# The second MoE's output products, pairs 2 and 3: from direct accumulation in PSUM to Strassen products of two quads, summed in SBUF

## The chip, the cores and the metric

One Trainium2 chip, one of its cores. The metric is the device time of one execution, in microseconds. Three timed runs of the kernel before took 842.42, 842.51 and 843.38 us; the profiled execution took 843.36 us. The engines named below: PE multiplies matrices and writes PSUM; DVE (vector), ACT (scalar) and POOL (GpSimd) work on elements; SP issues the DMAs.

## The reference

An attention with softmaxes over q and k and no score matrix, then two feed-forward layers, each 512 to 2048 to 512 over 2304 tokens:

```
q_s = softmax(q, axis=-1);  k_s = softmax(k, axis=seq)
x = q_s @ (k_s.T @ v)                              # 4 x 8 heads, 576 x 64 -> 2304 x 512
x = softplus(x @ moe_w_in) @ moe_w_out             # "first MoE"
out = elu(x @ moe2_w_in) @ moe2_w_out              # "second MoE"
```

All is float32.

## The kernel before

**Tiles.** Tokens go in six blocks of 384 (3 x 128), two blocks to a *pair* (p = 0, 1, 2 in the code, pairs 1 to 3 in the text). The 2048 inner columns go in eight *quads* of 256 (f = 0 to 7). The program is `for m in MoEs: for p in pairs: for f in quads`, 48 quads. Accuracy comes from splitting each float32 operand x into a high part (a cast to fp32r, by ACT) and a low part (x minus the high part, by DVE), and from three matmuls per product: high x high, high x low, low x high.

**Input products** (`add_up`, L791): for one quad and one pair, a Strassen scheme (Winograd's form) of seven products instead of eight, numbered 1, 2, 6, 5, 3, 7, 4 in PE's order. Each is six matmuls of 384 columns (L811) into the banks `ub`, `ua` or `uc`. ACT copies intermediate states of `ub` into `s` tiles (L824), DVE adds them to `ua` and `uc` for h (L845). The seven sums of x ("forms", `add_forms`) are made once per pair, in `xf`; those of w_in once, and for the second MoE they lie in DRAM (`wfd`) and are loaded per quad in pairs 2 and 3.

**Activation** (`add_elu`, L914): ACT computes relu(-h) and exp (L921, L925), DVE subtracts 1 (L929) and takes max(h, 0) + u for g (L933). `add_g` splits g, 768 columns for each of two row groups j, into `gh` (ACT, L940) and `gl` (DVE, L944).

**Output products** (`add_down`, L984): per quad, 2 x 2 x 3 groups of three matmuls of 512 columns (L1016) add to six PSUM banks `acc`, one per 128 tokens, which stay open over all eight quads of a pair. `add_store` then copies the banks out and stores them. A quad's output products are put between the next quad's input products. w_out's high and low parts (`wo`, 1 MB) lie in DRAM (`wod`) and are loaded per quad.

**Order.** Every operation is a *step* with an engine, an assumed duration, its operands and a ring of buffers (`rings`, L207). `Plan.order` plays all steps through once when the program is built and always takes, per engine, the step that can start soonest, ties by how late it may start; a step's lateness comes from due times given to PE's products and from a table of priorities (`PRI`, L1080). The result is one fixed order per engine, and each engine then runs its own instructions strictly in turn.

Of the kernel before, what the change touches and what calls it, by code (L numbers as in the profile page):

```python
# [147 lines left out]
def t_pool(n):  # L148
    return 0.15 + n / 476
# [7 lines left out]
def attention_moe_moe_kernel(  # L157
# [257 lines left out]
    def add_q(t, hps, behind=()):  # L415
# [26 lines left out]
        eng = POOL if early else DVE  # L442

        @step(eng, 1.1 if early else t_dve(n), r=[qm], w=[qk])
        def _(eng=eng):
            (nc.gpsimd if eng == POOL else nc.vector).tensor_tensor(
                flat(), flat(), T[qm][:, :N].to_broadcast([P, N, D]), op=ALU.subtract
            )
# [535 lines left out]
    def add_down(m, p, f):  # L984

        wk = ("wo", m, "o", f) if p == direct(m, 0, f) else ("wo", m, "o", f, p)
        t0 = after_quad(m, p, f)
# [6 lines left out]
        for (i, j, r), at in zip(order, fill):  # L994
# [11 lines left out]
                make=[(ak, f"acc{half}")] if first else [], due=t0 + at + 0.01, line=("acc", half, r),  # L1006
            )
            def _(col=col, j=j, hk=hk, lk=lk, ak=ak, first=first, whole=whole, gk=gk, w32=w32):
# [6 lines left out]
                for n, (g, a) in enumerate(((hk, 0), (hk, 1), (lk, 0))):  # L1015
# [4 lines left out]
                    )  # L1020

    def add_store(m, p):
# [22 lines left out]
        for half in range(2):  # L1045
            for r in range(R):
# [21 lines left out]

                @step(DMA, t_dma(P * DM * 4), r=[sk, ("y2", m)] if both else [sk], w=[] if m else [yk], after=LAT)
# [82 lines left out]

# [37 lines left out]
```

## Time and profile before

| what | value |
|---|---|
| median of three timed runs | 842.51 us |
| profiled execution, its time | 843.36 us |
| its span, first to last instruction | 841.3 us |
| PE busy, share of the span | 821.2 us, 98% |
| weight loads (beside PE) | 721.3 us |
| DVE busy | 590.1 us, 70% |
| ACT busy | 534.2 us, 63% |
| POOL busy | 6.1 us, 1% |
| TensorE clock granted | 0.999 of 2.4 GHz |
| DMA | 186.37 MB, 222 GB/s over the span |

How to read it: a row's duration is how long one instruction was under way. Instructions of one engine overlap, matmuls above all, so what one costs is the distance between starts. Times in windows and timelines count from the span's start. "xN" is a number of instructions.

### The profile page before, as it was taken

How to read it: one execution, taken by the hardware profiler on the slowest of the kernel's cores; microseconds unless marked ns; L12 is line 12 of the kernel's file. 1: busy time of each engine (PE TensorE's matmuls, PEld its weight loads, DVE VectorE, ACT ScalarE, POOL GpSimd, SP SyncE). 2: the span in 40 equal slices, each digit the busy share in tenths (PEclk: the TensorE clock that was granted, in tenths of full speed). 3: DMA queues.
4: the chain of work that ended last, by engine and by line, in shares of the span. 5: the costliest groups of instructions: out<-in, count | busy, mean ns of one | idle time of the engine just before them, and what ended most of it. 6: DMA issues, size and time to landing. Idle time of an engine off the chain costs nothing.

```text
span 841.3 us, 11929 instructions
## 1 busy us (share of the span) xinstructions
PE 821.2 (98%) x4678; PEld 721.3 (86%) x4678; DVE 590.1 (70%) x910; ACT 534.2 (63%) x786; POOL 6.1 (1%) x28
## 2 busy tenths in 40 slices
PE   5799999999999999999999999999999999999998
PEld 4466788889989999999999999899888899888896
DVE  7889999988888768776776786776544556533433
ACT  3877988886887757656655665665534456534443
POOL 2000000000000000000000000000000000000000
PEclk9999999999999999999999999999999999999999
DMA  9687775537885654687756689673765453763532
GB/s 283 165 280 248 216 261 194 199 100 238 263 310 181 236 205 161 221 303 267 250 178 230 261 300 338 257 295 143 250 234 216 179 232 139 255 232 138 187 139 76
DMA packets 63575, 186.37 MB, mean 222 GB/s; under 512 B 17952, under 2 KB 27168, under 8 KB 54560
## 3 DMA queue, kind: packets, MB, share of 16 engines
q1 hardware_dynamic: 63520, 185.61, 63.2%
q8 instruction: 37, 0.61, 0.3%
q14 instruction: 18, 0.15, 0.1%
HBM read 131.07 MB, written 54.53 MB: 221 GB/s over the span
## 4 chain that ended last, share of the span: by engine, by line
PE 83%; DVE 9%; ACT 5%; DMA 2%; issue 2%; ACTq 0%; DVEq 0%; SPq 0%
PE acc L1016 27%; PE ub L811 21%; PE acc L978 15%; PE uc L811 11%; PE ua L811 5%; PE px L507 1%; DMA raw_i<-in_moe_w_in_dram 1%; DMA raw_o<-in_moe_w_out_dram 1%; DVE mt L331 1%; PE pk L375 1%; DVE wf_i L731 1%; PE up L872 1%; ACT kvbd L401 1%; DVE ti_o L655 1%; PE pq L491 1%
## 5 line engine op out<-in xcount | busy, mean ns | idle before, releaser
L811 PE MATMUL ub<-xf,wf_i 128*128 128x384 f32 x1104 | 226.7, 340 | 0.4 <-ACT s L824 0.3
L1016 PE MATMUL acc<-wo_o,gh 128*128 128x512 f32 x720 | 226.0, 395 | 0.0
L811 PEld LDWEIGHTS ub<-xf,wf_i 128*128 128x128 f32 x1104 | 193.4, 188 | 16.5 <-ACT s L824 2.8
L845 DVE TENSOR_TENSOR h<-uc,s 128x384 f32<-128x384 f32 x92 | 51.1, 555 | 143.4 <-PE uc L811 135.0
L1016 PEld LDWEIGHTS acc<-wo_o,gh 128*128 128x128 f32 x720 | 132.5, 188 | 18.8
L1016 PE MATMUL acc<-wo_o,gl 128*128 128x512 f32 x360 | 142.5, 396 | 0.0
L824 ACT COPY s<-ub 128x384 f32<-128x384 f32 x138 | 65.9, 478 | 106.8 <-PE ub L811 106.5
L811 PE MATMUL uc<-xf,wf_i 128*128 128x384 f32 x552 | 112.2, 338 | 0.6 <-ACT g L893 0.6
L978 PE MATMUL acc<-gh,wo_o 128*128 128x512 f32 (+1 forms) x512 | 111.4, 339 | 0.0
L811 PEld LDWEIGHTS uc<-xf,wf_i 128*128 128x128 f32 x552 | 96.6, 188 | 8.2 <-ACT g L893 1.4
L940 ACT CAST gh<-g 128x768 fp32r<-128x768 f32 x92 | 77.1, 839 | 37.8 <-DVE g L933 37.1
L944 DVE TENSOR_TENSOR gl<-g,gh 128x768 fp32r<-128x768 f32 x92 | 87.8, 954 | 18.2 <-ACT gh L940 17.8
L978 PEld LDWEIGHTS acc<-gh,wo_o 128*128 128x128 f32 x512 | 83.2, 188 | 7.1
L1016 PEld LDWEIGHTS acc<-wo_o,gl 128*128 128x128 f32 x360 | 67.5, 187 | 14.4
L978 PE MATMUL acc<-gl,wo_o 128*128 128x512 f32 (+1 forms) x256 | 65.4, 336 | 0.0
L811 PE MATMUL ua<-xf,wf_i 128*128 128x384 f32 x276 | 55.8, 336 | 0.0
L811 PEld LDWEIGHTS ua<-xf,wf_i 128*128 128x128 f32 x276 | 48.0, 188 | 1.4 <-ACT xq L497 0.3
L933 DVE SCALAR_TENSOR_TENSOR g<-h,u 128x768 f32<-128x768 f32 x48 | 45.9, 957 | 1.4
L978 PEld LDWEIGHTS acc<-gl,wo_o 128*128 128x128 f32 x256 | 39.1, 188 | 5.3
L921 ACT ACTIVATE u<-h 128x768 f32<-128x768 f32 x48 | 40.7, 848 | 4.5 <-DVE h L845 2.7
L731 DVE TENSOR_TENSOR wf_i<-st_i,wf_i 128x1024 fp32r<-128x1024 f32 x30 | 36.6, 1221 | 8.1 <-ACT wf_i L727 7.9
L925 ACT ACTIVATE u<-u 128x768 f32<-128x768 f32 x48 | 40.7, 847 | 1.1
(98 smaller groups left out, 937.1 us busy)
## 6 DMA issues: line engine op xcount, KB each, us to landing
wo_o<-wod SPq DMA_DIRECT2D x30, 1024.0 KB, 6.8
wf_i<-wfd SPq DMA_DIRECT2D x16, 1792.0 KB, 7.3
raw_i<-in_moe_w_in_dram SPq DMA_DIRECT2D x16, 1024.0 KB, 6.5
raw_o<-in_moe_w_out_dram SPq DMA_DIRECT2D x16, 1024.0 KB, 7.4
wod<-wo_o SPq DMA_DIRECT2D x16, 1024.0 KB, 6.2
wfd<-wf_i SPq DMA_DIRECT2D x8, 1792.0 KB, 9.0
r_i<-w32i SPq DMA_DIRECT2D x24, 512.0 KB, 5.5
w32i<-ti_i SPq DMA_DIRECT2D x14, 512.0 KB, 5.5
```

What stands on the lines that cost most here:

```text
L331: top = lambda o, x, y: nc.vector.tensor_tensor(o, x, y, op=ALU.max)
L731: nc.vector.tensor_tensor(view(1, lo, n, c), get(), view(0, lo, n, c).bitcast(F32), op=ALU.subtract)
L811: nc.tensor.matmul(ps[:, :BLK], T[wk][:, lo : lo + P], T[xk][:, (2 * c + kc) * BLK : (2 * c + kc + 1) * BLK], start=(i in first and kc == ...
L824: nc.scalar.copy(new(sk), T[key][:, :BLK])
L845: nc.vector.tensor_tensor(T[hk][:, half * BLK : (half + 1) * BLK], T[key][:, :BLK], T[sk], op=ALU.add)
L921: nc.scalar.activation(new(uk), T[hk], AF.Relu, scale=-1.0)
L925: nc.scalar.activation(T[uk], T[uk], AF.Exp, scale=-1.0)
L933: nc.vector.scalar_tensor_tensor(new(gk), T[hk], 0.0, T[uk], op0=ALU.max, op1=ALU.add)
L940: nc.scalar.copy(new(hk), T[gk])
L944: nc.vector.tensor_tensor(new(lk), T[gk], T[hk].bitcast(F32), op=ALU.subtract)
L978: nc.tensor.matmul(ps, T[wk][:, lo : lo + P], T[g][:, cols], start=(first and n == 0 and starts), stop=(f == NQ - 1 and j == 1 and n == 2) ...
L1016: nc.tensor.matmul(ps, T[g][:, col : col + P], T[wk][:, (2 * a + j) * DM : (2 * a + j + 1) * DM], start=(first and n == 0), stop=(f == NQ ...
```

## The change

For pairs 2 and 3 of the second MoE (`fast(m, p)`: m = 1 and p > 0) the output products too become Strassen products, over two quads at a time (step c = 0 to 3, quads 2c and 2c+1):

- `add_g_fast` replaces `add_g`: g stays float32 in its buffer. Per quad POOL makes the sums of its four blocks (four subtractions of 384 columns), ACT and DVE split each of seven forms into a tile `dx`, which takes both quads' parts.
- `add_down_fast` replaces `add_down`: for each form, in the order 1, 2, 6, 5, 3, 7, 4, three groups (one per 128 tokens) of six matmuls of 256 columns into a bank `db`, `da` or `dc`. After each group the bank's present sum is added to half a row of the output in SBUF (`Y`), by DVE, or copied there by ACT where it is the first. Banks `db` and `dc` are written on after that. Rows go to DRAM at the last step; there is no `add_store` for these pairs.
- `add_w_down`, in pair 1: POOL makes four sums of w_out's blocks, ACT and DVE split them, and five DMAs per quad write the seven blocks, high and low, to DRAM (`wdd`) instead of the one DMA to `wod`. `load_w_down` loads them in five tiles per step, from rings "wo", "ti" and "st".
- Due times: input forms of fast pairs are spread evenly over a quad; the last quad of pair 1 is due over twice the time.
- `t_pool` and the table `PRI` get new numbers. `ON_POOL` names what POOL may do; attention's four subtractions of the first block stay there as before, all else in the table is on DVE.

Before:

```
        for n, (g, a) in enumerate(((hk, 0), (hk, 1), (lk, 0))):
            nc.tensor.matmul(ps, T[g][:, col : col + P],
                T[wk][:, (2 * a + j) * DM : (2 * a + j + 1) * DM], ...)      # 512 columns, L1016
```

The diff, its core:

```
 def t_pool(n):
-    return 0.15 + n / 476
+    return 0.03 + n / 476
...
+    fast = lambda m, p: m == 1 and p > 0
...
+    ON_POOL = {"qs": (0,), "qn": (), "ts": (), "st": ()}
...
+        if m:
+            early("so")
+            return add_w_down(f, rk)
...
+    RAW = (("g", "g"), ("gh", "gl"), ("gh", "gl"), ("gh", "gl"))
+    DOWN = (1, 2, 6, 5, 3, 7, 4)
+    TILES = (((1, 2), "wo"), ((6,), "ti"), ((5, 3), "wo"), ((7,), "ti"), ((4,), "st"))
...
+    def add_g_fast(p, f):
...
+        def form(i, src):
+            key, hold, view = src
+            xk, hk, lk = ("dx", p, c, i), ("dh", p, c, i, n), ("dl", p, c, i, n)
+            part = lambda a: T[xk][:, (2 * a + n) * BLK : (2 * a + n + 1) * BLK]
+            ring = "sx" if i in (2, 5, 7) and (c < 2 or p == NPAIR - 1) else "raw"
...
+                nc.scalar.copy(part(0), view())
...
+                nc.vector.tensor_tensor(part(1), view(), part(0).bitcast(F32), op=ALU.subtract)
...
+                nc.gpsimd.tensor_tensor(to[2](), one[2](), two[2](), op=ALU.subtract)
...
+        form(1, b(1, 1))
+        t1 = diff(b(1, 2), b(1, 1), b(1, 1))
+        form(2, b(2, 1))
+        t2 = diff(b(2, 2), t1, (tk, tk, lambda: T[tk]), True)
+        form(6, t2)
+        form(5, t1)
+        form(3, b(2, 2))
+        form(7, diff(b(2, 2), b(1, 2), b(1, 2)))
+        form(4, diff(b(2, 1), t2, b(2, 1)))
+
+    def add_down_fast(p, c):
...
+        goes = {1: (0, 0), 2: (0, 0), 6: (0, 1), 5: (1, 1), 3: (1, 0), 7: (1, 1), 4: (0, 1)}
+        where = {1: "b", 6: "b", 5: "b", 3: "b", 2: "a", 7: "c", 4: "c"}
...
+                    ps = new(key) if starts else T[key]
+                    for q in range(2):
+                        for m, (x, a) in enumerate(((0, 0), (0, 1), (1, 0))):
+                            lo = (2 * x + q) * BLK + r * P
+                            at = slot * 2 * DM + (2 * a + q) * HALF
+                            nc.tensor.matmul(
+                                ps[:, :HALF], T[xk][:, lo : lo + P], T[wk][:, at : at + HALF],
...
+                eng = ACT if fresh else DVE
...
+                    if fresh:
+                        nc.scalar.copy(to, of)
+                    else:
+                        nc.vector.tensor_tensor(to, of, to, op=ALU.add)
...
-        k00=97, q00=38, k01=54, q01=13, k02=167, q02=154, k03=94, q03=54, k10=9, q10=83, k12=24, q12=11,
+        k00=18, q00=61, k01=27, q01=58, k02=208, q02=54, k03=165, q03=21, k10=-15, q10=14, k12=8, q12=29,
...
```

**What moves in the order.** Names are tiles; in them the numbers are, for `ub_2_6` pair and quad (p = 2, f = 6), for `xf_2_1` pair and form, for `acc_2_1_0` pair, block, row group, for `dx_1_6` step and form, for `db_1_0` step and row group, for `Y_0_1` block and row group; the last number counts tiles.

PE in the middle of pair 3, before: input forms of quad 6 and output groups of quad 5.

```order
L811 MATMUL ub_2_6_7470<-xf_2_1_6619,wf_i_2_7337 128x384 x6
L811 MATMUL ua_2_6_7480<-xf_2_2_6627,wf_i_2_7337 128x384 x6
L1016 MATMUL acc_2_0_0_6889<-wo_o_2_7387,gh_2_5_0_7451 128x512 x2
L1016 MATMUL acc_2_0_0_6889<-wo_o_2_7387,gl_2_5_0_7461 128x512
L811 MATMUL ub_2_6_7470<-xf_2_6_6645,wf_i_2_7337 128x384 x6
L1016 MATMUL acc_2_0_1_6905<-wo_o_2_7387,gh_2_5_0_7451 128x512 x2
L1016 MATMUL acc_2_0_1_6905<-wo_o_2_7387,gl_2_5_0_7461 128x512
L1016 MATMUL acc_2_0_2_6911<-wo_o_2_7387,gh_2_5_0_7451 128x512 x2
L1016 MATMUL acc_2_0_2_6911<-wo_o_2_7387,gl_2_5_0_7461 128x512
L811 MATMUL ub_2_6_7470<-xf_2_5_6667,wf_i_2_7337 128x384 x6
```

PE at the same place, after: input forms of quad 5 and products 6, 5 and 3 of step 1.

```order
L896 MATMUL ub_2_5_8025<-xf_2_1_6956,wf_i_2_7867 128x384 x6
L1122 MATMUL db_1_0_7934<-wd_1_1_7767,dx_1_6_7926 128x256 x6
L896 MATMUL ua_2_5_8049<-xf_2_2_6967,wf_i_2_7867 128x384 x6
L1122 MATMUL db_1_1_7946<-wd_1_1_7767,dx_1_6_7926 128x256 x6
L1122 MATMUL db_1_2_7966<-wd_1_1_7767,dx_1_6_7926 128x256 x6
L896 MATMUL ub_2_5_8025<-xf_2_6_7048,wf_i_2_7867 128x384 x6
L1122 MATMUL db_1_0_7934<-wd_1_2_7817,dx_1_5_7944 128x256 x6
L1122 MATMUL db_1_1_7946<-wd_1_2_7817,dx_1_5_7944 128x256 x6
L896 MATMUL ub_2_5_8025<-xf_2_5_7068,wf_i_2_7867 128x384 x6
L1122 MATMUL db_1_2_7966<-wd_1_2_7817,dx_1_5_7944 128x256 x6
L1122 MATMUL db_1_0_7934<-wd_1_2_7817,dx_1_3_7984 128x256 x6
```

Groups of three matmuls of 512 columns have become groups of six of 256; one bank `db_1_0` is written by product 6, then by 5, then by 3, with two or three groups of other work between.

DVE at that place in pair 3, before: the halves of h, u and g of quad 5 and 6, and `gl`.

```order
L845 TENSOR_TENSOR h_2_6_0_7494<-ua_2_6_7480,s_1_2_6_7487 128x384
L944 TENSOR_TENSOR gl_2_5_1_7496<-g_2_5_1_7478,gh_2_5_1_7489 128x768
L845 TENSOR_TENSOR h_2_6_1_7551<-uc_2_6_7538,s_1_2_6_7523 128x384
L929 TENSOR_SCALAR u_2_6_0_7545<-u_2_6_0_7545 128x768
L933 SCALAR_TENSOR_TENSOR g_2_6_0_7563<-h_2_6_0_7494,u_2_6_0_7545 128x768
L845 TENSOR_TENSOR h_2_6_1_7551<-uc_2_6_7538,s_1_2_6_7509 128x384
L944 TENSOR_TENSOR gl_2_6_0_7576<-g_2_6_0_7563,gh_2_6_0_7568 128x768
L929 TENSOR_SCALAR u_2_6_1_7574<-u_2_6_1_7574 128x768
L933 SCALAR_TENSOR_TENSOR g_2_6_1_7595<-h_2_6_1_7551,u_2_6_1_7574 128x768
```

DVE at that place, after: step 1's additions to the rows `Y` and low parts of its forms, among h, u and g of quad 4.

```order
L1141 TENSOR_TENSOR Y_0_0_7675<-db_1_0_7934,Y_0_0_7675 128x256
L1065 TENSOR_TENSOR dx_1_5_7944<-g_2_2_0_7653,dx_1_5_7944 128x384
L1065 TENSOR_TENSOR dx_1_5_7944<-g_2_3_0_7822,dx_1_5_7944 128x384
L1141 TENSOR_TENSOR Y_0_1_7688<-db_1_1_7946,Y_0_1_7688 128x256
L1141 TENSOR_TENSOR Y_0_2_7629<-db_1_2_7966,Y_0_2_7629 128x256
L930 TENSOR_TENSOR h_2_4_1_7994<-uc_2_4_7974,s_1_2_4_7941 128x384
L1065 TENSOR_TENSOR dx_1_3_7984<-g_2_2_1_7726,dx_1_3_7984 128x384
L1016 TENSOR_SCALAR u_2_4_0_7981<-u_2_4_0_7981 128x768
L1065 TENSOR_TENSOR dx_1_3_7984<-g_2_3_1_7881,dx_1_3_7984 128x384
L1020 SCALAR_TENSOR_TENSOR g_2_4_0_8013<-h_2_4_0_7896,u_2_4_0_7981 128x768
L930 TENSOR_TENSOR h_2_4_1_7994<-uc_2_4_7974,s_1_2_4_7910 128x384
L1141 TENSOR_TENSOR Y_0_0_7675<-da_1_0_7986,Y_0_0_7675 128x256
```

The `gl` of 768 columns is gone; per quad seven subtractions of 384 and ten or eleven additions of 256 columns stand in turn with h, u and g.

PE at the start of pair 2 of the second MoE, before: the last output group of pair 1, then quad 1's input forms.

```order
L1016 MATMUL acc_0_1_2_4867<-wo_o_5614,gl_0_7_1_5799 128x512
L811 MATMUL ub_1_1_5873<-xf_1_1_5625,wf_i_1_5732 128x384 x6
L811 MATMUL ua_1_1_5885<-xf_1_2_5633,wf_i_1_5732 128x384 x6
L1016 MATMUL acc_1_0_0_5896<-wo_o_1_5786,gh_1_0_0_5854 128x512 x2
L1016 MATMUL acc_1_0_0_5896<-wo_o_1_5786,gl_1_0_0_5862 128x512
L811 MATMUL ub_1_1_5873<-xf_1_6_5648,wf_i_1_5732 128x384 x6
L1016 MATMUL acc_1_0_1_5912<-wo_o_1_5786,gh_1_0_0_5854 128x512 x2
L1016 MATMUL acc_1_0_1_5912<-wo_o_1_5786,gl_1_0_0_5862 128x512
L1016 MATMUL acc_1_0_2_5918<-wo_o_1_5786,gh_1_0_0_5854 128x512 x2
```

PE at the same place, after: quads 1 and 2, up to the first product of step 0.

```order
L1225 MATMUL acc_0_1_2_4892<-wo_o_5702,gl_0_7_1_5898 128x512
L896 MATMUL ub_1_1_5978<-xf_1_1_5714,wf_i_1_5905 128x384 x6
L896 MATMUL ua_1_1_5989<-xf_1_2_5722,wf_i_1_5905 128x384 x6
L896 MATMUL ub_1_1_5978<-xf_1_6_5736,wf_i_1_5905 128x384 x6
L896 MATMUL ub_1_1_5978<-xf_1_5_5767,wf_i_1_5905 128x384 x6
L896 MATMUL ub_1_1_5978<-xf_1_3_5796,wf_i_1_5905 128x384 x6
L896 MATMUL uc_1_1_6037<-xf_1_7_5804,wf_i_1_5905 128x384 x6
L896 MATMUL uc_1_1_6037<-xf_1_4_5834,wf_i_1_5905 128x384 x6
L896 MATMUL ub_1_2_6058<-xf_1_1_5714,wf_i_1_5976 128x384 x6
L896 MATMUL ua_1_2_6073<-xf_1_2_5722,wf_i_1_5976 128x384 x6
L896 MATMUL ub_1_2_6058<-xf_1_6_5736,wf_i_1_5976 128x384 x6
L1122 MATMUL db_0_0_6096<-wd_0_0_5880,dx_0_1_5961 128x256 x6
```

Ten input forms follow each other with no output group between, since step 0 needs both quads' g.

## Rows read from the trace of the kernel before

**Rows 1.** The page, part 1: busy us, share of the span, instructions.
```profile
PE 821.2 (98%) x4678; PEld 721.3 (86%) x4678; DVE 590.1 (70%) x910; ACT 534.2 (63%) x786; POOL 6.1 (1%) x28
```

**Rows 2.** Busy us (and instructions) per engine in stages; clock, DMA share, GB/s.
```profile
core 0: us, PE busy (x) PEld busy (x) DVE busy (x) ACT busy (x) POOL busy (x), PEclk, DMA share, GB/s
0.00:40.00 40.00, 25.80 (x292) 18.42 (x292) 34.11 (x87) 25.08 (x41) 5.57 (x24) 1.00 0.76 225
...
63.00:150.00 87.00, 86.00 (x449) 67.10 (x448) 86.04 (x131) 73.34 (x102) 0.13 (x1) 1.00 0.72 231
...
453.20:578.70 125.50, 125.50 (x639) 113.48 (x638) 91.18 (x136) 81.03 (x118) 0.00 (x0) 1.00 0.72 267
578.70:704.50 125.80, 125.78 (x626) 112.87 (x625) 62.63 (x87) 61.61 (x91) 0.00 (x0) 1.00 0.56 209
```

**Rows 3.** Timeline of PE, one quad of pair 2: start, us, line, tiles, shape, count.
```profile
641.69 1.20 PE L811 MATMUL ua<-xf,wf_i 128*128 128x384 f32 x6
642.73 0.63 PE L1016 MATMUL acc<-wo_o,gh 128*128 128x512 f32 x2
...
657.37 0.33 PE L811 MATMUL ua<-xf,wf_i 128*128 128x384 f32 x1
```

**Rows 4.** Timelines of PE and its weight loads, first MoE, 249.68 to 250.9 us.
```profile
249.68 0.86 PE L978 MATMUL acc<-gh,wo_o 128*128 128x512 f32 x4
250.37 0.51 PE L978 MATMUL acc<-gl,wo_o 128*128 128x512 f32 x2
250.72 1.20 PE L811 MATMUL uc<-xf,wf_i 128*128 128x384 f32 x6
...
249.91 0.31 PEld L978 LDWEIGHTS acc<-gh,wo_o 128*128 128x128 f32 x2
```

**Rows 5.** Timeline of DVE: instructions that follow each other at once, two places.
```profile
64.65 0.43 DVE L731 TENSOR_TENSOR wf_i<-ti_i,wf_i 128x256 fp32r<-128x256 f32 x1
64.98 0.43 DVE L711 TENSOR_TENSOR st_i<-ti_i 128x256 f32<-128x256 f32 x1
...
642.99 0.56 DVE L845 TENSOR_TENSOR h<-ua,s 128x384 f32<-128x384 f32 x1 [1.03 <-PE ua L811]
643.47 0.95 DVE L944 TENSOR_TENSOR gl<-g,gh 128x768 fp32r<-128x768 f32 x1
644.34 0.95 DVE L599 TENSOR_TENSOR ts<-sx,sx 128x768 f32<-128x768 f32 x1
```

**Rows 6.** Groups by line and shape: DVE, then ACT (busy us, mean ns, idle before).
```profile
L845 DVE TENSOR_TENSOR h<-uc,s 128x384 f32<-128x384 f32 x92 | 51.1, 555 | 143.4 <-PE uc L811 135.0 <-ACT u L921 4.5 <-ACT g L893 3.7
...
L929 DVE TENSOR_SCALAR u<-u 128x768 f32<-128x768 f32 x48 | 26.6, 555 | 13.5 <-ACT u L925 13.5
...
L755 DVE TENSOR_TENSOR wo_o<-r_o,wo_o 128x1024 fp32r<-128x1024 f32 x10 | 12.2, 1221 | 1.7 <-ACT wo_o L751 1.7
...
L921 ACT ACTIVATE u<-h 128x768 f32<-128x768 f32 x48 | 40.7, 848 | 4.5 <-DVE h L845 2.7
```

**Rows 7.** Timelines of DVE and POOL at 16.8 us: one instruction of each.
```profile
17.52 0.56 DVE L476 TENSOR_TENSOR q<-q,qd 128x384 f32<-128x384 f32 x1
...
16.80 0.83 POOL L446 TENSOR_TENSOR q<-q,qm 128x384 f32<-128x384 f32 x1 [0.93 <-DVE qd L461]
```

**Rows 8.** Waits of PE's weight loads: who for whom, us, times, longest.
```profile
PEld ub L811 <- ACT s L824: 2.8, 7, 0.8
```

**Rows 9.** DMA issues: tiles, count, KB each, us to landing.
```profile
wo_o<-wod SPq DMA_DIRECT2D x30, 1024.0 KB, 6.8
...
wod<-wo_o SPq DMA_DIRECT2D x16, 1024.0 KB, 6.2
```

**Rows 10.** Chain that ended last, its end: start, us, what.
```profile
826.57 10.94 PE acc L1016 x48
...
837.53 0.43 DVE y L1067
...
837.98 0.37 ACT y L1067
```

More of the change, by code (lines that the diff above doesn't have):

```diff
@@ L264, in after_quad, with elementwise @@
         return start[quads[i]] if i < len(quads) else end
+    ON_POOL = {"qs": (0,), "qn": (), "ts": (), "st": ()}
+    def elementwise(kind, where, n):
+        if where in ON_POOL[kind]:
+            return POOL, t_pool(n), nc.gpsimd
+        return DVE, t_dve(n), nc.vector
     kload = {}
@@ L441, in add_q, with _ @@
         N = 2 * R * G
[L442 to L446, printed above, removed]
+        eng, dur, nce = elementwise("qs", t, n)
+        @step(eng, dur, r=[qm], w=[qk])
+        def _(nce=nce):
+            nce.tensor_tensor(
                 flat(), flat(), T[qm][:, :N].to_broadcast([P, N, D]), op=ALU.subtract
@@ L595, in diff @@
             key = ("ts", m, p, i)
-            @step(DVE, t_dve(2 * BLK), r=[*one[0], *two[0]], make=[(key, "ts")], hold=[one[1], two[1]], line="ts")
+            eng, dur, nce = elementwise("ts", (m, p), 2 * BLK)
+            @step(eng, dur, r=[*one[0], *two[0]], make=[(key, "ts")], hold=[one[1], two[1]], line="ts")
             def _():
-                nc.vector.tensor_tensor(new(key), one[2](), two[2](), op=ALU.subtract)
+                nce.tensor_tensor(new(key), one[2](), two[2](), op=ALU.subtract)
             return ts(i)
@@ new lines, in load_w_down, with _ @@
+    def load_w_down(p, c):
+        first = 0
+        for n, (forms, ring) in enumerate(TILES):
+            key, lo, k = ("wd", p, c, n), first * 2 * DM, len(forms) * 2 * DM
+            first += len(forms)
+            @step(
+                DMA, t_dma(P * k * 4), r=[("wdd", c, f, x) for f in (2 * c, 2 * c + 1) for x in range(5)],
+                make=[(key, ring)], after=LAT, behind=[last["wo"]], line=("wd", ring),
+            )
+            def _(key=key, lo=lo, k=k):
+                nc.sync.dma_start(out=new(key, F32R).bitcast(F32), in_=T["wdd", c][:, lo : lo + k])
@@ L917, in add_elu @@
         hs = [("hp", 1, p, f, j, half) for half in range(2)]
+        blocks = [("b", p, f, j, half) for half in range(2)] if fast(1, p) else []
+        ring = (RAW[f % 4][j] if fast(1, p) else "g")
         @step(ACT, t_act(N2), r=hs, hold=[hk], make=[(uk, "u")], line="u")
@@ L1130, in attention_moe_moe_kernel @@
             add_w_out(m, f, load_words(m, p, "o", f))
-        else:
+        elif not fast(m, p):
             load_w_out(m, p, f)
+        elif f % 2:
+            early("wd")
+            load_w_down(p, f // 2)
         if (m, p, f) in ahead:
```

157 lines of the change are left out of this document (139 added, 18 removed).

## The prediction

> **What bounds the kernel now.** I read the page first: PE is busy 821.2 of 841.3 us, DVE 590.1, ACT 534.2, POOL 6.1 [rows 1]. The reader is to see that PE has no holes after the first three slices. A share of 98% doesn't say what a change in one stage is worth, so I then cut the span into stages [rows 2]. From 453.2 us on the second MoE runs, one pair of token blocks per 125 to 126 us. In pairs 1 and 2 (to 704.5) PE is busy to within 0.02 us of each stretch; pair 3 repeats pair 2's work. In pair 2 DVE works 62.6 of 125.8 us, ACT 61.6, POOL nothing. There PE's own instructions set the end, so time is won by fewer PE nanoseconds and lost where another engine makes PE wait. Before 150 us it is different: DVE is busy 86.0 of 87 us between 63 and 150, and PE loses 14.2 us in the first 40.
>
> Third, PE's row of instructions through one quad of pair 2 [rows 3]: 641.69 to 657.37 us, 15.68 us, without an idle gap: seven forms of six 384-column matmuls and twelve groups of three 512-column ones. A form takes 641.69 to 642.73, 1.04 us, 173 ns per matmul. Seven forms take 7.30, which leaves 8.38 us for the 36 wide matmuls, 233 ns each. The length of a PE row (0.33 for one matmul) is no use here, since matmuls overlap; only distances between starts are.
>
> **The change part by part.**
>
> *Products.* Two quads of pairs 2 and 3 gave 72 matmuls of 512 columns, 16.76 us. They now give 7 x 3 x 6 = 126 of 256 columns. A 256-column matmul stands in the first MoE, after each 512-column one [rows 4]: three of either kind take 249.68 to 250.72, 1.04 us; less 3 x 0.233 that is 114 ns for the narrow one; the last two, 250.37 to 250.72, take 0.35, so 117. I take 117: 126 x 0.117 = 14.74 us. Saved: 2.02 us per two quads. Two pairs hold eight such steps: -16.2 us. What could spoil this price is the weight load: each takes 188 ns, longer than 117. But the two loads for a narrow and the next wide matmul together take 0.31 us [rows 4], so the second starts some 0.12 after the first: loads overlap. A run of nothing but narrow matmuls doesn't stand in the trace; its bounds are 114 ns and 188.
>
> *DVE work.* Starts of DVE instructions that follow each other at once [rows 5]: 384 elements 0.48 us, 256 elements 0.34, 768 elements 0.87. Per two quads four subtractions gl go (3.5 us); in come 14 of 384 elements (6.7) and 21 additions of a 256-column bank to its row (7.1; 9 of them at the first step of a pair, where ACT copies the other 12). What stays is six h (2.9), four u (taken as a 384, since both rows last about 555 ns: 1.9) and four g (3.5) [rows 6]. Sum 22.1 us against PE's 29.3: 75%, where it was about 12 of 31.4. So DVE stays below PE. In the order the pieces of a form are subtracted one or more products ahead, and each bank is added with one or two PE groups between it and its next writer, some 1.5 to 2.5 us of cover. If DVE is later than that, PE waits one for one.
>
> *The second half of pair 2* is the thin place. There the seven forms go through two "raw" buffers (elsewhere "sx" takes three of them), so a form's casts start only when the product two before has left PE; and DVE also makes pair 3's input forms, 11 x 0.87 = 9.6 us. DVE then has 2 x 22.1 + 9.6 = 53.8 of 58.6 us, 92%. Bounds: 0 if all is early, 8 if each of the 14 products waits 0.6 us (a cast and a subtraction that start only when the buffer comes free). I take +2.0.
>
> *POOL.* 64 subtractions of 384 elements, 0.83 us each by such a row [rows 7], 6.6 us per two quads: alone no bound. Do DVE and POOL disturb each other? The trace has one DVE instruction with both inputs in SBUF that begins inside a POOL one: at 17.52, when POOL's ran 16.80 to 17.63, and it took 0.56, as its like do [rows 7]. An overlap of 0.1 us shows little. Bounds: 0, or all 64 x 0.83 = 53 us handed to DVE. I take +0.8: DVE has 7 us spare per two quads, so nearly all of it is absorbed. The Trainium skill's page "SBUF — State Buffer", section "Who interferes with whom", says that a DVE instruction with two SBUF inputs and a GpSimd instruction that reads SBUF lock each other out for a whole instruction. The short overlap above does not bear it out, nor does it refute it; by the row the sum stays, by the rule it becomes that of rival 2.
>
> *Pair 1 to pair 2.* The Strassen products wait until two quads have their g, so ten input forms now stand alone on PE. Two of them write the bank that ACT is just copying: a wait of 0.4 us each (2.8 us in 7 times) [rows 8]. The first product also waits for h, u, g and a cast of the second quad, about 5 us, covered by five forms of 1.04. I take +1.1 (0.4 to 3).
>
> *Pair 1* (453.2 to 578.7): per quad POOL gets four sums, ACT and DVE one pass over 1024 elements each, a DVE row of 1.22 us [rows 6]. DVE has 91.2 of 125.5 and gets 9.8: 80%. The queue writes 1792 KB instead of 1024 [rows 9], 6.3 MB more over this stretch, 50 GB/s on top of 267; its share goes from 0.72 to about 0.86. Written blocks are read only a pair later, but tiles are held longer. I take +0.5 (0 to 4). In pairs 2 and 3 loads rise from 2048 to 3584 KB per two quads: share from 0.56 to about 0.70, which the trace carries elsewhere (0.72 in pair 1).
>
> *Order table and start.* All priorities are new and attention's loads come in another order. DVE and the input transfers bind there, not POOL's four subtractions, which stay. Nothing in a row prices it: 0, bounds -2.5 and +2.5 (a sixth of PE's 14.2 us of idling).
>
> *The end.* The last step's 21 groups follow the last input forms without filling; before it 48 matmuls stood like that for 10.94 us [rows 10]. Between the last form and the product that needs its g now lie nine groups of 0.70, 6.3 us; the chain of h, ACT's two passes over u, DVE's one, g, cast and subtraction is 0.56 + 0.85 + 0.85 + 0.56 + 0.95 and twice some 0.5 for 384 elements, 4.8 plus hand-overs [rows 5, 6]. Covered. The last eviction is one addition instead of two halves one behind the other, 0.43 + 0.37: -0.4.
>
> **Sum.** -16.2 + 2.0 + 0.8 + 1.1 + 0.5 + 0 - 0.4 = -12.2 us. The profiled execution took 843.4 us (841.3 of span, 2.1 around it); that gives 831.2. The median of the timed runs is 0.9 lower, so 830.3.
>
> **The rivals.**
> 1. *PE remains the bound*, with waits of a few us in all: 830.3, own range 824 to 836. For it: PE without a gap in all of [rows 2], DVE at 75%. Against it: the 92% in half a pair. Chance 0.72.
> 2. *DVE becomes the bound in the changed pairs, the gain is halved*: POOL's 6.6 us fall on DVE, 28.7 of 29.3 us, and in the second half of pair 2 67 of 58.6: +8.4 there instead of 2.8 for both terms, 835.9, and up to 0.8 more at each of the other six steps, 840.7. Against it: the undisturbed 0.56 row. Chance 0.16.
> 3. *Slower than before*: the lock-out by POOL at its worst. A bank is written by two products in a row three times per step (6 then 5, 5 then 3, 7 then 4); if its addition sits behind a DVE instruction that POOL shuts out, PE waits 0.83 each time, 2.5 us per step, 15 over six steps, and 8.4 in the thin place: 843.4 - 16.2 + 23.4 + 1.6 - 0.9 = 851. It decides from 2.0 us per step, about a third of POOL's time reaching PE. The cover of 1.5 us and more speaks against it. Chance 0.05.
> 4. *Narrow matmuls run at the pace of the weight load*: 1008 x (188 - 117) ns = 71.6 us, 902. The break-even is 16.76 / 126 = 133 ns. The overlapping loads speak against it. Chance 0.02.
> 5. *The saving is real but the start or pair 1's fuller DMA takes it back*: 841 to 844. For it: the start is bound by DVE and transfers, and the table moves all of it; against it: nothing there gains work. Chance 0.05.
>
> **How the numbers follow.** The likeliest is 830.3 us. The lower end is the median less the full saving, the table's best 2.5 and the end's 0.4, plus 0.4 of waits, 823.8, so 824; the upper end takes in the larger part of rival 2: 839. Measurements of this kernel can't tell less than about 0.2%, 1.7 us: faster means below 840.8. Rivals 1 and 2: 0.88. Within: most of 5, 0.04. Slower: 3, 4 and the rest of 5, 0.08.
>
> **What would show it.** Starts of the 256-column product groups 0.70 us apart (six matmuls); above 0.80 rival 4 holds. Quads of pairs 2 and 3 every 14.7 us instead of 15.7. PE's waits should name DVE rows of the second half of pair 2 and ACT's s copies at the first step; waits that name the row additions all through pair 3, with DVE rows of two SBUF inputs longer than 0.56 or later beside POOL rows, would show rival 2 or 3. POOL rows much above 0.83 us would spoil the cover of forms 6 and 4. The forecast is wrong if pairs 2 and 3 take over 245 us together, or if the second MoE begins more than 3 us off 453.2.

## The result, and the profile after

The changed kernel takes 851.4 us (four runs, 851.41 to 851.62), the kernel before 842.9 in the same session (842.42 to 843.38): a ratio of 1.0102, 95% interval 1.0084 to 1.0119. It is slower by 1%, where 830.3 us were forecast. The profiled execution took 851.4 us, 849.6 of it span.

The page's first part, after:

```profile
PE 817.5 (96%) x5110; PEld 736.0 (87%) x5110; DVE 700.4 (82%) x1136; ACT 561.2 (66%) x889; POOL 117.6 (14%) x124
```

Against [rows 1] PE is no longer busy nearly all the time (96%), DVE rises from 590 to 700 us, and GpSimd (POOL) from 6 to 118. That is 111 us for 64 subtractions and 32 sums that the planner had priced at 64 x 0.84 and 32 x 0.57, 72 us. By stages (busy us and instructions of each engine, granted clock, DMA share, GB/s):

```profile
63.00:150.00 87.00, 86.97 (x448) 67.90 (x447) 85.47 (x129) 71.55 (x100) 0.13 (x1) 1.00 0.75 245
452.80:580.20 127.40, 126.76 (x638) 112.87 (x637) 101.24 (x140) 84.21 (x122) 26.24 (x28) 1.00 0.85 303
580.20:696.00 115.80, 113.31 (x748) 109.97 (x747) 91.59 (x160) 70.99 (x132) 29.73 (x25) 1.00 0.75 276
700.80:711.20 10.40, 6.26 (x28) 5.63 (x27) 8.74 (x12) 4.55 (x7) 5.99 (x5) 0.67 0.06 24
706.30:710.40 4.10, 4.09 (x19) 4.09 (x20) 3.19 (x5) 3.24 (x6) 0.49 (x1) 0.50 0.00 0
822.00:837.40 15.40, 11.55 (x76) 10.37 (x75) 14.54 (x24) 4.91 (x11) 10.03 (x8) 0.89 0.32 104
```

The first row is as in [rows 2]. Pair 1 takes 127.4 us (125.5 before). From 580.2 to 696 PE has lost 2.5 us. The fourth and the last row are the places where most of the time went: PE works 6.3 of 10.4 us, then 11.6 of 15.4, while DVE has 8.7 and 14.5, and the granted clock falls to 0.67 and 0.89. The fifth row is a part of the fourth.

Where nothing waits the products are as cheap as forecast, or nearly. PE in pair 2 (start, time, repeats), to be read against [rows 3]:

```profile
664.40 1.21 PE L896 MATMUL ua<-xf,wf_i 128*128 128x384 f32 x6
665.45 0.87 PE L1122 MATMUL dc<-wd,dx 128*128 128x256 f32 x6
666.16 1.20 PE L896 MATMUL ub<-xf,wf_i 128*128 128x384 f32 x6
...
678.84 1.20 PE L896 MATMUL ua<-xf,wf_i 128*128 128x384 f32 x6
...
693.99 0.69 PE L896 MATMUL ua<-xf,wf_i 128*128 128x384 f32 x3
```

Six 256-column matmuls go from 665.45 to 666.16, 0.71 us or 118 ns each; two quads go from 664.40 to 693.99, 29.6 us, where two quads of before take 31.4. That is 1.8 us saved per step (2.02 forecast), 14.2 in eight.

What makes PE wait there? The waits of PE from 575 us on (total, times, longest; "issue" is a wait for which the trace names nobody):

```profile
PE db L1122 <- DVE Y L1141: 3.7, 2, 3.6
PE db L1122 <- issue: 2.9, 1, 2.9
PE ub L896 <- ACT s L909: 2.7, 5, 0.8
PE uc L896 <- DVE h L930: 2.5, 2, 1.7
...
```

DVE is named in most, by its additions of a bank to a row (Y) and by h. Both read PSUM and keep their length: 45 Y rows and 7 h rows begin while a GpSimd subtraction is under way, and they take 0.41 to 0.43 and 0.54 to 0.55 us like the others. Instructions that read SBUF alone do not. Groups of DVE in pairs 2 and 3 (busy us, mean ns of one; behind the bar the idle time in front):

```profile
L1065 DVE TENSOR_TENSOR dx<-g,dx 128x384 fp32r<-128x384 f32 x96 | 65.2, 702 | 2.0 <-ACT dx L1061 1.7
L1020 DVE SCALAR_TENSOR_TENSOR g<-h,u 128x768 f32<-128x768 f32 x34 | 35.6, 1046 | 0.4
L1141 DVE TENSOR_TENSOR Y<-db,Y 128x256 f32<-128x256 f32 x72 | 29.2, 418 | 10.2 <-PE db L1122 9.6
L1016 DVE TENSOR_SCALAR u<-u 128x768 f32<-128x768 f32 x34 | 23.0, 676 | 3.4 <-ACT u L1012 3.0
...
L930 DVE TENSOR_TENSOR h<-uc,s 128x384 f32<-128x384 f32 x33 | 18.2, 553 | 23.2 <-PE uc L896 12.9 <-ACT h L915 9.6 <-ACT dx L1061 0.7
L1065 DVE TENSOR_TENSOR dx<-t,dx 128x384 fp32r<-128x384 f32 x16 | 13.9, 870 | 2.2 <-ACT dx L1061 2.1
```

And the groups of GpSimd, by the same view:

```profile
L1075 POOL TENSOR_TENSOR g<-g,g 128x384 f32<-128x384 f32 x16 | 21.6, 1350 | 0.0
...
L1075 POOL TENSOR_TENSOR t<-g,g 128x384 f32<-128x384 f32 x16 | 20.1, 1254 | 3.7 <-DVE g L1020 3.5
```

dx, the subtraction priced by a 0.56 us row [rows 7], takes 0.70 and 0.87 on average; u takes 0.68 where it took 0.555 [rows 6]; g takes 1.05, and 0.95 where nothing is beside it (e2). GpSimd's subtractions take 1.25 to 1.35 us, not 0.83. The h and Y rows are as short as ever. The timeline at the worst place shows how the long ones come about:

```profile
700.42 1.29 DVE L604 TENSOR_TENSOR xf<-sx,xf 128x768 fp32r<-128x768 f32 x1
700.85 1.72 POOL L1075 TENSOR_TENSOR t<-g,g 128x384 f32<-128x384 f32 x1
701.63 2.62 DVE L1065 TENSOR_TENSOR dx<-g,dx 128x384 fp32r<-128x384 f32 x2
702.54 1.30 POOL L1075 TENSOR_TENSOR g<-g,g 128x384 f32<-128x384 f32 x1
703.80 2.98 POOL L1075 TENSOR_TENSOR g<-g,t 128x384 f32<-128x384 f32 x2
704.18 0.74 DVE L1141 TENSOR_TENSOR Y<-db,Y 128x256 f32<-128x256 f32 x2
704.84 1.08 DVE L613 TENSOR_TENSOR ts<-sx 128x768 f32<-128x768 f32 x1
705.85 0.41 DVE L1141 TENSOR_TENSOR Y<-db,Y 128x256 f32<-128x256 f32 x1
```

DVE's xf (0.95 us alone) takes 1.29, and its two dx 2.62 instead of about 1.03; GpSimd beside them takes 1.72 and 1.30 where its shortest rows are 1.02. The two engines take turns, a whole instruction at a time: the second dx ends at 704.25, 0.41 us after GpSimd's row of 702.54. So it is everywhere. Of the 112 dx rows 32 are lengthened, to 1.16 us on average, and each of the 32 ends 0.41 or 0.42 us after a GpSimd row does, wherever it began; the other 80 take 0.55 to 0.58. Only at 704.18 does DVE come to the Y additions, and the third of them has one more instruction of 768 elements (ts, for pair 3's input forms) in front of it. PE, over the same time:

```profile
699.27 1.59 PE L1122 MATMUL db<-wd,dx 128*128 128x256 f32 x12
...
701.76 0.97 PE L896 MATMUL ub<-xf,wf_i 128*128 128x384 f32 x4 [0.55 <-DVE xf L604]
706.31 1.65 PE L1122 MATMUL db<-wd,dx 128*128 128x256 f32 x6 [3.58 <-DVE Y L1141]
707.76 2.55 PE L1122 MATMUL da<-wd,dx 128*128 128x256 f32 x11
```

PE waits 3.58 us, until the Y of 705.85 has ended (706.26), and then runs at half the clock, 1.2 GHz (0.50 granted over 706.3 to 710.4): six matmuls from 706.31 to 707.76 take 242 ns each.

From the same trace I summed, over all of PE's matmuls from 575 us on, what each start is late against 174 ns (384 columns) and 117 ns (256): 21.7 us, of which some 4 are matmuls at half the clock. Before it was 0.6.

| place | forecast | after | e2 (below) |
|---|---|---|---|
| products, eight steps | -16.2 | -14.2 | |
| pair 1 to 2, 597 to 608 us | +1.1 | +3.5 | 2.8 |
| second half of pair 2, its last step, 701 to 711 | +2.0 | +6.9 | 1.1 |
| GpSimd elsewhere: 612, 737 to 747, 797 | +0.8 | +4.6 | 0.1 |
| last step, 822 to 837 | -0.4 with the end | +6.7, end -0.5 | 0.8 |
| pair 1 | +0.5 | +1.9 | |
| before 452.8 | 0 | -0.4 | |

The column "after" sums to +8.5, less the 0.6 of waits that before had: 7.9, against 8.3 of span (849.6 less 841.3).

### The profile page after: what moved, and what is told of

Same layout as the page of the kernel before. It is cut to its first block, busy times and chain, and to the rows that moved or that the text cites. A ratio compares the mean times of both kernels' runs of the same rounds, so it can differ in the third digit from the quotient of the medians.

```text
span 849.6 us, 13401 instructions
## 1 busy us (share of the span) xinstructions
PE 817.5 (96%) x5110; PEld 736.0 (87%) x5110; DVE 700.4 (82%) x1136; ACT 561.2 (66%) x889; POOL 117.6 (14%) x124
## 4 chain that ended last, share of the span: by engine, by line
PE 77%; DVE 13%; ACT 5%; DMA 2%; issue 2%; POOL 1%; SPq 0%; DVEq 0%; POOLq 0%; ACTq 0%
PE ub L896 19%; PE acc L1185 14%; PE acc L1225 11%; PE uc L896 10%; PE db L1122 6%; PE ua L896 5%; DVE dx L1065 3%; PE acc L1220 2%; PE dc L1122 2%; PE up L957 2%; PE px L519 2%; PE da L1122 2%; DVE g L1020 2%; PE pk L385 1%; DVE Y L1141 1%
## 5 line engine op out<-in xcount | busy, mean ns | idle before, releaser
L1225 PE MATMUL acc<-wo_o,gh 128*128 128x512 f32 x336 | 106.3, 397 | 0.0
L1122 PE MATMUL db<-wd,dx 128*128 128x256 f32 x576 | 79.2, 287 | 6.6 <-DVE Y L1141 3.7
L1122 PEld LDWEIGHTS db<-wd,dx 128*128 128x128 f32 x576 | 76.4, 194 | 7.6 <-DVE Y L1141 4.4
L1061 ACT CAST dx<-g 128x384 fp32r<-128x384 f32 x96 | 46.7, 511 | 50.7 <-DVE g L1020 22.1
L1225 PEld LDWEIGHTS acc<-wo_o,gh 128*128 128x128 f32 x336 | 61.6, 188 | 9.0
L1031 DVE TENSOR_TENSOR gl<-g,gh 128x768 fp32r<-128x768 f32 x60 | 57.2, 953 | 14.5 <-ACT gh L1027 14.2
L1065 DVE TENSOR_TENSOR dx<-g,dx 128x384 fp32r<-128x384 f32 x96 | 65.2, 702 | 2.0 <-ACT dx L1061 1.7
L1225 PE MATMUL acc<-wo_o,gl 128*128 128x512 f32 x168 | 66.5, 396 | 0.0
L1027 ACT CAST gh<-g 128x768 fp32r<-128x768 f32 x60 | 50.2, 837 | 17.1 <-DVE g L1020 15.3
L806 POOL TENSOR_TENSOR sto<-r_o 128x256 f32<-128x256 f32 x16 | 12.6, 789 | 314.8 <-DMA r_o<-w32o 293.6
```

The costliest lines, as they stand in the source:

```text
L1027: nc.scalar.copy(new(hk), T[gk])
L1061: nc.scalar.copy(part(0), view())
L1065: nc.vector.tensor_tensor(part(1), view(), part(0).bitcast(F32), op=ALU.subtract)
L1122: nc.tensor.matmul(ps[:, :HALF], T[xk][:, lo : lo + P], T[wk][:, at : at + HALF], start=(starts and q == 0 and m == 0), stop=(q == 1 and m ...
L1225: nc.tensor.matmul(ps, T[g][:, col : col + P], T[wk][:, (2 * a + j) * DM : (2 * a + j + 1) * DM], start=(first and n == 0), stop=(f == NQ ...
```

## The experiments

Theory A: GpSimd's subtractions and DVE's instructions that work from SBUF shut each other out, so DVE comes late to h and Y, and PE waits. Theory B: DVE is full or its queue badly ordered, and GpSimd is innocent. Theory C: GpSimd's instructions are longer than priced, and so the casts of the forms made from them are late. D and E came up on the way.

**e1 and e2: GpSimd works less, or writes only.** Order and planned times are those of the changed kernel. In e1, where a sum has a tile of its own (t, 16 of the 64), GpSimd also sets that tile's other 336 columns to 0.

```
-  nc.gpsimd.tensor_tensor(to[2](), one[2](), two[2](), op=ALU.subtract)
e1: +  nc.gpsimd.tensor_tensor(to[2]()[:, :48], one[2]()[:, :48], two[2]()[:, :48], ...)
e2: +  for _ in range(2): nc.gpsimd.memset(to[2](), 0.0)
```

> The 64 block subtractions on GpSimd work on 48 of their 384 columns (the forms made from them are then not the reference's); order and all else as in the changed kernel (851.4 us). Theory A (GpSimd's subtractions and DVE's instructions with two SBUF inputs shut each other out, and DVE comes late to the row additions): the dx subtractions, 0.70 us on average, go back to 0.55, g from 1.05 to 0.95; PE's waits at 702, 742 and 830 us and the half-clock stretches behind them (about 15 us) mostly vanish: 833 to 840 us. Theory B (DVE is simply full and its queue in a bad order; the long DVE rows are waits that the trace books as work): 848 to 852. Theory C (GpSimd's own length, 1.31 instead of 0.84 us, makes the casts of forms 6, 7 and 4 late): 833 to 840 as well; e2 tells C from A.

> Each of the 64 subtractions on GpSimd becomes two memsets of its 384 result columns, which write and read nothing (the forms are then not the reference's). GpSimd stays busy for an estimated 0.9 us per place (a 128-column memset takes 0.205). Theory A with the lock on reads: dx back to 0.55 us although GpSimd works beside it, 833 to 840 us. Theory A with a lock on any GpSimd access: dx stays near 0.70, 846 to 852. Theory C: GpSimd's length is nearly what it was, 845 to 851. Theory B: 848 to 852.

e1: 835.7 us, 0.9908 (0.9887 to 0.9929) of before. e2: 835.4 us, 0.9907 (0.9892 to 0.9921). Both are 16 us below the changed kernel. In e1 GpSimd's rows average 0.38 us. In e2 GpSimd stays busy, 0.86 to 0.94 us per place, though it only writes; DVE's groups of e2 from 575 us on:

```profile
L1065 DVE TENSOR_TENSOR dx<-g,dx 128x384 fp32r<-128x384 f32 x96 | 50.8, 552 | 2.5 <-ACT dx L1061 1.9
L1020 DVE SCALAR_TENSOR_TENSOR g<-h,u 128x768 f32<-128x768 f32 x34 | 32.4, 952 | 0.4
...
L1016 DVE TENSOR_SCALAR u<-u 128x768 f32<-128x768 f32 x34 | 20.1, 590 | 4.0 <-ACT u L1012 3.4
...
L1065 DVE TENSOR_TENSOR dx<-t,dx 128x384 fp32r<-128x384 f32 x16 | 8.6, 553 | 0.7 <-ACT dx L1061 0.5
```

GpSimd's memsets, by the same view:

```profile
L1076 POOL MEMSET g<- 128x384 f32 x96 | 40.2, 432 | 201.3 <-DVE dx L1065 188.2 <-PE ub L896 10.4
L1076 POOL MEMSET t<- 128x384 f32 x32 | 15.0, 470 | 0.9
```

dx is back at 0.552 with GpSimd at work beside it, g at 0.952. u stays somewhat long: six of them begin while a memset is under way and take 0.65 to 0.89 us, the others 0.55 or 0.56. This refutes B: DVE has the same queue in the same order. It leaves little room for C, since GpSimd's 0.9 us per place is close to the 1.02 of an undisturbed subtraction. Theory A holds, for instructions with two SBUF inputs with the conflict on GpSimd's reads; u, with one input, is held up by GpSimd's writes too. PE's lateness after 575 us falls from 21.7 to 4.8 us (last column of the table).

**e9: the same conflict where DVE has room.** Two GpSimd subtractions per g in the kernel before; its other engines' order is unchanged.

```
+  if m and p:
+      for x in range(2): nc.gpsimd.tensor_tensor(spare, g[:, :BLK], g[:, BLK:], op=ALU.subtract)
```

> The kernel before, in its own order, with two subtractions of 384 elements on GpSimd for each g of pairs 2 and 3 (64 in all, both inputs in SBUF, the result never read). They start when g is there, about when ACT casts it and DVE then makes gl from two SBUF inputs. Theory A (mutual lock): gl, 0.953 us before, becomes 1.3 to 1.6 where GpSimd runs; h, which reads PSUM, stays at 0.55; GpSimd's rows are 1.02 or more; and PE doesn't wait, since DVE has only 62.6 of 125.8 us of work there: 841.5 to 844 us. Theory B (long rows are an effect of a full DVE queue): gl stays 0.953.

843.4 us, 0.9997 (0.9988 to 1.0007): no change. But the rows change. DVE and GpSimd at 641.9 us:

```profile
641.92 2.12 POOL L951 TENSOR_TENSOR spare<-g 128x384 f32<-128x384 f32 x2 [1.62 <-DVE g L934]
642.65 0.56 DVE L846 TENSOR_TENSOR h<-ua,s 128x384 f32<-128x384 f32 x1 [0.87 <-PE ua L812]
643.13 1.72 DVE L945 TENSOR_TENSOR gl<-g,gh 128x768 fp32r<-128x768 f32 x1
```

and DVE's groups over pairs 2 and 3:

```profile
L945 DVE TENSOR_TENSOR gl<-g,gh 128x768 fp32r<-128x768 f32 x34 | 42.1, 1237 | 6.4 <-ACT gh L941 5.6
...
L846 DVE TENSOR_TENSOR h<-uc,s 128x384 f32<-128x384 f32 x32 | 17.8, 557 | 91.0 <-PE uc L812 91.0
```

GpSimd's rows, by the same view:

```profile
L951 POOL TENSOR_TENSOR spare<-g 128x384 f32<-128x384 f32 x64 | 79.7, 1246 | 535.9 <-DVE g L934 533.4
```

gl was 0.955 and is 1.24 on average, 1.72 here, where GpSimd's second subtraction is under way; h at 642.65, with one input in PSUM, stays at 0.56 right beside GpSimd. GpSimd's own rows fall in two groups, 40 of about 1.02 us and 24 of about 1.6. So the exclusion is there without any of the change's other parts, and it costs nothing as long as DVE has half its time free.

**e5: the thin place alone.** e2's memsets only where `p == 1 and f >= 4`.

> As e2 (memsets in place of GpSimd's subtractions, so these forms are not the reference's), but only in the second half of pair 2, 16 of the 64. Theory A: the 6.9 us that PE loses between 700 and 711 us in the changed kernel (851.4) become about 1.1 as in e2, and the later waits (737 to 747, 797, 822 to 837 us: 10.6) stay: 844 to 847.5. Theory D (DVE's lag there is only handed on, and the next waits grow by what this one loses): 849 to 852.

848.2 us, 1.0052 (1.0037 to 1.0067): 3.2 below the changed kernel, less than A's 4 to 7 and outside both ranges. In the trace the place itself does what A says, 6.85 us of lateness become 1.14. But the one after it, at 733 to 744 us, grows from 2.9 to 4.4, since PE's matmuls behind its wait there now run at half the clock too; pair 2 began 2.0 us later (582.3 against 580.2), ahead of anything that this kernel changes; and the last step loses 1.3 us less. -5.7 + 1.5 + 2.0 - 1.3 is -3.5, the difference of the spans (846.1 and 849.6). The place is A's; D, a lag handed on whole, does not hold. What is left over comes from places that the edit does not touch.

**e3, e10, e11, e8: the subtractions on DVE.** e3 moves them and leaves the priorities as they were; the planner makes its order from these. e10 is e3 with the planner's priorities set anew for it (nine numbers: the second MoE's input forms and rows, the products, the sums and loads of w_out's blocks, and two new ones for u and g and for the forms made from g). e11 is e3 with u's subtraction of 1 on ACT in pairs 2 and 3, old priorities. e8 has u on ACT and priorities of its own.

```
e3:  -  @step(POOL, t_pool(BLK), r=[one[0], two[0]], ...     nc.gpsimd.tensor_tensor(
     +  @step(DVE, t_dve(BLK), r=[one[0], two[0]], ...       nc.vector.tensor_tensor(
e10: -  x10=-105, x11=42, x12=-16, y=47, dn=-8, wd=16, so=-3
     +  x10=-151, x11=6, x12=10, y=47.1, dn=-3.8, wd=177.1, so=-57.1, gf=-9.2, eu=-13.3
e11: -  nc.vector.tensor_scalar(T[uk], T[uk], -1.0, None, op0=ALU.add)
     +  nc.scalar.activation(T[uk], T[uk], AF.Copy, bias=-1.0)
```

> The 64 subtractions run on DVE instead of GpSimd, planned as DVE work. DVE gets 64 x 0.48 = 31 us more over eight steps, but nothing blocks it. Theory A: dx 0.55 us; per step DVE has 22.1 + 3.8 = 26 of PE's 29.4 us, in the second half of pair 2 61 of 58.6, so some 3 to 8 us of waits stay there: 838 to 845 us, below 851.4. Theory B (DVE's load is the cause): the load rises by a sixth, 855 to 880. Theory C: as A.

> e3 (the 64 subtractions on DVE, u's subtraction on DVE too) with priorities set anew as in e8: one of the two differences between e3 (852.1) and e8 (838.8). If the order is what e3 lacked: 837 to 843. If DVE's load is (1.9 us per step): 846 to 851. In between: both.

> e3 with u's subtraction of 1 on ACT, priorities as in the changed kernel: the other of the two differences. If DVE's load is what e3 had too much of: 838 to 844. If the order is: 846 to 851.

> As e3 (the 64 subtractions on DVE, nothing on GpSimd beside the products), with the subtraction of 1 from u in pairs 2 and 3 on ACT and priorities set anew. DVE per step 22.1 + 3.8 - 1.9 = 24.0 us of PE's 29.4. If e3's 852 came from DVE's sum in the tight places alone: 834 to 843. If it came from the order of DVE's queue there, whatever its sum: 846 to 853.

| kernel | us | of before (95%) |
|---|---|---|
| e3, moved | 852.1 | 1.0106 (1.0088 to 1.0123) |
| e11, and u on ACT | 849.2 | 1.0074 (1.0051 to 1.0097) |
| e10, and the order anew | 839.7 | 0.9949 (0.9931 to 0.9967) |
| e8, both | 838.8 | 0.9944 (0.9928 to 0.9961) |

e3 was a miss: A had expected 838 to 845. Without GpSimd DVE's rows are short again, but the order comes from priorities that were set with the subtractions on GpSimd. PE's waits from 575 us on in e3:

```profile
PE da L1122 <- DVE Y L1141: 3.4, 1, 3.4
PE ub L896 <- DVE xf L604: 3.1, 1, 3.1
PE uc L896 <- DVE h L930: 2.1, 3, 0.7
...
```

The same view of e10:

```profile
PE ub L896 <- ACT s L909: 2.8, 5, 0.6
PE uc L896 <- DVE h L930: 1.4, 2, 0.7
PE da L1122 <- ACT dx L1061: 0.9, 1, 0.9
...
```

In e3 two single waits of more than 3 us stand out, one of them for pair 3's input forms (xf) beside the last step of pair 2. In e10 the longest is 0.9. The work is the same; over 690 to 718 us DVE is busy 26.4 us in e3 and 26.7 in e10, of 28. So it is not the sum of DVE's work but who stands behind what in its queue that decides: new priorities alone give 12.4 us (e3 to e10), the 1.9 us per step that ACT takes over give 2.8 with the old priorities (e3 to e11). With new ones (e10 to e8) they give 0.9, which the intervals do not tell from nothing. e8 by itself came out in the range that stood for DVE's sum; since its order was new as well, it could not tell the two apart, and e10 and e11 do.

**e4, e6, e7: GpSimd stays, the planner is told.** e4 gives the planner GpSimd's measured times. e6 adds the exclusion, as the `port` mark that the planner knows, on GpSimd's steps and on DVE's SBUF-only ones, priorities set anew; e7 adds u on ACT.

```
e4: -  @step(POOL, t_pool(BLK), r=[one[0], two[0]], ...
    +  @step(POOL, t_pool_two(BLK), r=[one[0], two[0]], ...                # 0.19 + n / 340
e6: +  @step(POOL, t_pool_two(BLK), port=True, r=[one[0], two[0]], ...     # 0.19 + n / 465
    +  @step(DVE, t_dve(BLK), port=True, r=[key, hk], w=[lk], ...          # and u, g, gl, xf, ts, w
```

> The planner is told 1.32 us for a block subtraction on GpSimd and 0.94 for a sum of w_out's blocks (it had 0.84 and 0.57; measured means 1.31 and 0.95), so it writes another order on all engines; the work is the same. Theory C: the order then fits the times, 833 to 842 us. Theory A: the blocks stay, wherever they fall, since DVE's lengths are still priced undisturbed: 844 to 856. Theory B: 846 to 856.

> All work as in the changed kernel, but the planner is told, in the second MoE, that GpSimd's instructions and DVE's with inputs in SBUF alone exclude each other (and 1.02 and 0.74 us for GpSimd's two kinds), and the priorities were set anew for it. So DVE's reads of PSUM should fall beside GpSimd's instructions. Theory A: dx near 0.55 to 0.60 us, GpSimd's subtractions near 1.02 to 1.15, most of the 21.7 us of waits gone: 834 to 843. Theory E (the exclusion itself, not its place, costs the time, since DVE must give up GpSimd's 64 x 1.0 us either way): 846 to 854.

> As e6, and the subtraction of 1 from u in pairs 2 and 3 on ACT instead of DVE (32 instructions, 0.48 us each by start to start, 1.9 us per step off DVE, and no GpSimd instruction beside them to wait for); priorities set anew. Theory A and DVE as the bound in the tight places: 1 to 4 us below e6: 832 to 840. Theory E: 844 to 852. If ACT (58% busy) becomes late instead: waits naming ACT rows, above e6.

e4: 853.6 us, 1.0123 (1.0101 to 1.0144): true lengths alone don't help, which speaks against C again. e6: 847.4, 1.0049 (1.0034 to 1.0063), outside what A gave for it and inside E. e7: 841.6, 0.9975 (0.9963 to 0.9986), between the two ranges; u on ACT gives 5.8 us here, twice the 2.8 without GpSimd. In e6 DVE's dx rows are hardly shorter than in the changed kernel:

```profile
L1069 DVE TENSOR_TENSOR dx<-g,dx 128x384 fp32r<-128x384 f32 x96 | 62.7, 674 | 4.8 <-ACT dx L1065 4.3
...
L1069 DVE TENSOR_TENSOR dx<-t,dx 128x384 fp32r<-128x384 f32 x16 | 15.8, 1010 | 0.2 <-ACT dx L1065 0.2
```

The mean of all 112 is 0.72 us, after 0.73; g and u are nearer to undisturbed (0.98 and 0.61). The planner kept the two apart only in part: per step GpSimd wants 8 x 1.02 us and DVE's SBUF-only work (14 dx, four u and four g by the starts) some 12, of 29.6. That the order can hide the conflict is not shown. Leaving GpSimd out is better both times that priorities were set for each: e10 is 7.7 us below e6, e8 2.8 below e7.

**e12: the sums too.** e8 with the `port` mark on the sums of w_out's blocks and DVE's work beside them in pair 1.

> e8, with the planner told of the exclusion for GpSimd's sums of w_out's blocks in pair 1 too (the only GpSimd work left beside DVE), priorities set anew. e8 lost 2.2 us in PE waits there (526 and 550 us): 835.5 to 838.5 if they came from the exclusion, 838 to 840 if from pair 1's added work as such.

838.3 us, 0.9937 (0.9923 to 0.9952), against e8's 838.8: no difference that these runs can tell. Pair 1's excess is not settled by it. e8, e10 and e12 are below both kernels with intervals clear of 1, by 0.5 to 0.6% of the kernel before.

## Why the prediction was wrong

- *Products*: mechanism right, size a little off: -14.2 instead of -16.2. The narrow matmul came at 118 ns, not 117, and two quads at 29.6 us, not 29.3. Rival 4 (188 ns) falls.
- *POOL, +0.8*: this step failed. It rested on one DVE row that began 0.1 us before the end of a GpSimd row [rows 7] and was as long as its like; both read a short operand spread over the row, not two full ones. Nor could that row have shown a conflict: in the changed kernel a dx that begins inside a GpSimd row ends 0.41 us after it, so one that begins 0.1 us before its end would be done after 0.52 us, within its usual 0.56. Real block subtractions took 1.02 us undisturbed, not 0.83. And they take DVE's time: over pairs 2 and 3 the rows of dx are 19.5 us longer than 112 x 0.552, those of g 3.2 and of u 4.1 (against 0.953 and 0.555), 26.8 in all. That is 0.42 us of DVE per GpSimd subtraction, where DVE itself would need 0.48 by its starts. GpSimd relieved DVE of little. The Trainium skill's page "SBUF — State Buffer", section "Who interferes with whom", gave the rule: an exclusive lock on a port pair that the two share, and for a DVE instruction with two SBUF inputs only where GpSimd reads; the traces agree (dx 0.55 beside memsets, up to 1.38 beside subtractions; gl 1.72 in e9).
- *"Nearly all of it is absorbed" by 7 us of spare DVE time per step*: the second half of the failed step. Spare time on average did not help where a queue is tight. e9 shows 79.7 us of the same conflict absorbed to nothing in a kernel that has DVE half idle; e2 shows that a GpSimd that reads nothing returns 16.0 us, e10 that DVE doing it all in another order returns 11.7. Cover of 1.5 to 2.5 us ahead of a bank is gone after two DVE instructions of 1.3 us each.
- *Second half of pair 2, +2.0 (0 to 8)*: the place was right, and 6.9 lies inside its bounds. Without the conflict it is 1.1 (e2). The price left out what follows a long wait: about 2 us at half the clock.
- *Pair 1 to 2, +1.1 (0.4 to 3)*: measured 3.5, and 2.8 without the conflict (e2). There PE is late by 0.73 us twice for the copy of a bank and by 0.88 a third time, for h. The 0.4 taken from [rows 8] was the mean of seven waits of which the longest had 0.8, and the wait for h was left out.
- *The end, -0.4*: wrong by 6.7. "Covered" did not count the Y additions of the last step, which stand in DVE's queue behind four dx of 1.36 us, 827.3 to 832.4, turn about with GpSimd's; PE then waits 2.9 us, by the times for the first of them: the trace names nobody, and that Y ended at 833.25, just before PE went on at 833.35. e2 loses 0.8 there.
- *Pair 1, +0.5 (0 to 4)*: 1.9. *Start*: as said, 452.8 against 453.2.
- *The rivals*: rival 3 gave 851 for the lock-out at its worst and stood at 0.05; the time came out there and the mechanism is its own, but not as it drew it. It had 2.5 us at each of six steps and 8.4 in the thin place; the traces show most steps with almost nothing and four places with long waits. The weight was set by a row that did not hold the case, with a stated rule on the other side.

The Trainium skill's page "GPSIMD Engine Reference", section "Engine selection", advises VectorE for elementwise work on a tile. e10 agrees: the same 64 subtractions on DVE, in an order made for it, are 7.7 us faster than e6 with GpSimd; with u on ACT the difference is 2.8 (e8 and e7).

Open: how much of pair 1's 1.9 us is the conflict with the sums, and whether some order could hide GpSimd's subtractions altogether.

## What to carry to other kernels

Before work is moved to GpSimd to relieve DVE, price it as DVE time: count the DVE instructions that read only SBUF in the stretch, and where they fill much of it, expect to pay nearly what DVE would have paid itself (here 0.42 of 0.48 us for each). A mean share of spare time says little about a queue; look at the tightest stretch, and at who waits behind the instruction that grows. And when work is moved between engines, have the priorities of the order set anew: with GpSimd out of the way that was worth 12.4 us here, and taking 1.9 us per step off the busy engine 2.8.

## What was not expected of the hardware

- A GpSimd subtraction of two full 384-element rows takes 1.02 us alone, 0.83 with one operand spread from 6 values [rows 7]; 256 elements take 0.74.
- Beside GpSimd's reads each lengthened DVE instruction waits for what is left of GpSimd's (a dx ends 0.41 us after it), and GpSimd for DVE's: 1.36 us per dx against 1.33 per subtraction where both are queued. The one-input u (0.555 alone) is held up as well, 1.26 at 695.6 us, and unlike dx also by memsets, up to 0.89 in e2.
- After PE had waited 3.58 us, its clock was granted at half for about 4 us (242 ns for a 256-column matmul); behind the waits of 0.3 to 0.8 us at 597 to 604 us it was not. The length of one wait did not decide it: behind 1.73 us at 744 us the clock stayed full in the changed kernel (1.00 over 744 to 748), and behind the same 1.73 us at 740.35 in e5 it fell (0.61 over 740.3 to 744.5).
